# Re-sequencing the opening of a fused retention and GELU-MLP kernel: banks of the state product, weight triggers, who evacuates x

## The chip, the cores and the metric

One core of a Trainium2 chip runs the kernel. The metric is the device time of one execution in microseconds. The records of each execution also give the core's span (first to last instruction, about 1.8 us shorter than the device time here) and the mean clock granted to TensorE, as a share of full speed.

## The reference, cut to what matters

```python
state = gamma * state + k_t v_t^T          # retention, per batch b and head h, 768 steps
y_t   = scale * q_t . state
x = y as (3072 tokens, 512)
h = x @ w_in                               # 512 -> 2048
out = gelu_tanh(h) @ w_out                 # 2048 -> 512
```

Batch 4, 8 heads of 64, 768 positions; fp32 inputs and output.

## The kernel before

The sequence is cut into 6 chunks c of 128 positions. For each chunk and batch b there are pieces of attention, called T, A, Y below, and then the MLP over the four batches together: M1 (`moe1`, 16 column blocks fc, each with a GELU on ScalarE) and M2 (`moe2`).

- T: transposes of scaled q and k on TensorE into a PSUM tile, then a copy to SBUF (`qkT`).
- A: products q k^T, then VectorE multiplies them with the decay mask (`a_sb`).
- Y: the products y = A v (plus q times state for c > 0), and s = k^T v in the same call. y is copied to SBUF as x, s is added to the state `st`, and GpSimd makes the decayed state `stg` for the next chunk.

In the code, `mm_` issues the products of a piece and `ev_` its evacuations from PSUM, `prep1` scales or converts one input, `decay` makes `stg`, and `hold` is a tiny GpSimd copy that waits for a weight and so holds back the loads of chunk 1. In the profiles `h_ps` are the products of M1 and `o_ps` those of M2, "o" and "h" for short.

PSUM is divided into groups of tiles: `att` 3, `o` 2, `h` 3. What the change touches:

```python
    def spin(n):                       # fillers: products of zeros that nobody reads
        ps = psum.tile([128, 512], F32, tag="h", bufs=3, name="spin_ps")
        ...
    def mm_Y(c, b):
        tag, bufs = ("o", 2) if c < 2 else ("att", 3)
        y_ps = psum.tile([128, NHP, 128], F32, tag=tag, bufs=bufs, name="y_ps")
        ...
        if c + 1 < NCk:
            s_ps = psum.tile([128, NHP, 128], F32, tag=tag, bufs=bufs, name="s_ps")
        ...
    # the opening, chunk 0 (cut)
    mm_A(0, 1); ev_A(0, 1); spin(2)
    PO.tensor_copy(out=misc[0:1, 1:2], in_=ld_tile("q", 0, 3)[0:1, 0, 0:1])
    load_w_in(0); load_w_in(1); prep1(PO, "k", 0, 3); load_w_in(2); load_w_in(3)
    mm_T(0, 2); ev_T(0, 2, AC); prep1(AC, "v", 0, 2); prep1(VE, "q", 0, 3)
    mm_Y(0, 1); ev_Y(0, 1, AC); ev_S(0, 0); spin(1)
    mm_A(0, 2); ev_A(0, 2); prep1(AC, "v", 0, 3); spin(3)
    mm_T(0, 3); ev_T(0, 3); mm_Y(0, 2); ev_Y(0, 2, AC)
    mm_A(0, 3); ev_A(0, 3); ev_S(0, 1); spin(1)
    moe1(0, 0, 0, half); moe1(0, 1, 0, half)
    mm_Y(0, 3); ev_Y(0, 3); ev_S(0, 2); ev_S(0, 3)
    for b in range(B): decay(0, b)
    ...
    # chunk 1 (cut)
    run1("T0"); moe1(0, NF - 1); run1("A0"); spin(3); run1("Y0 T1")
    ...
    zip_units(units, pieces(1, "T2 A2 Y2 T3 A3 Y3"))
```

## Time and profile before

| | before |
|---|---|
| median of 3 executions | 231.49 us (231.47 to 232.06) |
| the profiled execution | 233.13 us, span 231.3, clock 0.993 |
| TensorE busy | 219.0 us, 95% |
| slices of the clock row below 0.9 | one, at 11.6 to 17.3 us |

In the page's view of the span in 40 slices, the row for the clock has its only dip in the third slice, in tenths:

```profile
PEclk9979999999999999999999999999999999999999
```

The lines of the chain, the waits and the timelines are shown in the prediction.

### The profile page before, as it was taken

What the parts mean: (1) busy time and instruction counts of PE and PEld (TensorE: products, weight loads), DVE (VectorE), ACT (ScalarE), POOL (GpSimd) and SP (SyncE); (2) the same over time, 40 slices, a digit from 0 to 9 for tenths busy, and PEclk for the clock granted to TensorE, in tenths of its full rate; (3) what the DMA queues carried; (4) which work ended last, traced back from release to release, by engine and by line L of the source; (5) the groups of instructions that cost most, each with busy time, mean ns of one, the idle gap of its engine ahead of it and who ended that gap; (6) DMA issues with size and microseconds to landing.
All of it is one profiled execution on the core that took longest, in us unless ns stands there. A gap on an engine that the chain in (4) does not pass through costs nothing.

```text
span 231.3 us, 4076 instructions
## 1 busy us (share of the span) xinstructions
PE 219.0 (95%) x1669; PEld 119.0 (51%) x1669; DVE 84.1 (36%) x150; ACT 82.6 (36%) x161; POOL 78.7 (34%) x92
## 2 busy tenths in 40 slices
PE   7775999789999999999999999999999999999993
PEld 3434645678744554554544554445544445444453
DVE  3566205773000675645342445342434233200001
ACT  2642664647621111154511154511155412166220
POOL 3582388255940037940666546700000000000000
PEclk9979999999999999999999999999999999999999
DMA  7999799999995782299311199411110011200112
GB/s 178 288 183 206 140 268 254 204 194 235 203 251 163 192 207 89 66 246 204 83 45 48 45 229 253 111 45 48 47 45 3 0 45 50 90 1 0 43 51 91
DMA packets 83011, 29.74 MB, mean 129 GB/s; under 512 B 75568, under 2 KB 80048, under 8 KB 82992
## 3 DMA queue, kind: packets, MB, share of 16 engines
q1 hardware_dynamic: 65776, 17.94, 33.2%
q0 software_dynamic: 4224, 4.19, 11.2%
q10 hardware_dynamic: 12992, 7.34, 10.3%
q8 instruction: 13, 0.21, 0.4%
q14 instruction: 6, 0.05, 0.1%
HBM read 27.37 MB, written 6.29 MB: 146 GB/s over the span
## 4 chain that ended last, share of the span: by engine, by line
PE 86%; DVE 6%; DMA 5%; issue 1%; ACT 0%; SPq 0%; DVEq 0%
PE o_ps L342 36%; PE h_ps L322 35%; PE qkT_ps L175 4%; PE a_ps L193 3%; PE y_ps L228 3%; PE s_ps L240 3%; DMA q<-in_q_dram 2%; DMA k<-in_k_dram 2%; DVE a_sb L206 2%; PE y_ps L218 2%; DVE qkT L169 1%; DVE q L145 1%; PE spin_ps L112 1%; DVE st L259 1%; DVE xT L169 1%
## 5 line engine op out<-in xcount | busy, mean ns | idle before, releaser
L322 PE MATMUL h_ps<-xT,w_in 128*128 128x512 f16 (+2 forms) x504 | 89.7, 328 | 0.5 <-DVE xT L169 0.5
L342 PE MATMUL o_ps<-w_out,g 128*128 128x512 f16 (+1 forms) x400 | 87.8, 371 | 0.0
L331 ACT ACTIVATE g<-h_ps 128x512 f16<-128x512 f32 (+2 forms) x126 | 61.8, 496 | 64.4 <-PE h_ps L322 63.1
L322 PEld LDWEIGHTS <-w_in 128*128 128x128 f16 x504 | 44.7, 98 | 33.4 <-issue 0.6
L342 PEld LDWEIGHTS <-g 128*128 128x128 f16 x400 | 37.6, 98 | 39.0
L206 DVE TENSOR_TENSOR a_sb<-a_ps,mask 128x512 f16<-128x512 f32 x48 | 30.9, 686 | 28.4 <-PE a_ps L193 28.4
L363 ACT COPY o_sb<-o_ps 128x512 f32<-128x512 f32 x18 | 10.6, 586 | 67.2 <-PE o_ps L342 67.2
L268 POOL TENSOR_TENSOR stg<-st,cst 128x512 f32<-128x512 f16 x16 | 16.5, 1040 | 44.8 <-DVE st L259 39.7
L145 POOL TENSOR_TENSOR k<-k,cst 128x512 f16<-128x512 f32 x24 | 25.2, 1049 | 8.6 <-DMA k<-in_k_dram 8.6
L169 DVE CAST xT<-y_ps 128x512 f16<-128x512 f32 x21 | 14.5, 691 | 29.8 <-PE y_ps L228 29.8
L169 DVE COPY qkT<-qkT_ps 128x1024 f16<-128x1024 f16 x21 | 14.5, 692 | 26.4 <-PE qkT_ps L175 26.1
L145 POOL TENSOR_TENSOR q<-q,cst 128x512 f16<-128x512 f32 x20 | 20.9, 1045 | 9.3 <-DMA q<-in_q_dram 9.2
L259 DVE TENSOR_TENSOR st<-s_ps,stg 64x256 f16<-64x256 f32 x32 | 13.4, 418 | 0.5
L360 DVE COPY o_sb<-o_ps 128x512 f32<-128x512 f32 x5 | 3.5, 692 | 26.7 <-PE o_ps L342 26.7
L228 PE MATMUL y_ps<-a_sb,v 128*64 128x128 f16 x192 | 10.8, 225 | 1.9 <-DVE st L257 0.9
L193 PE MATMUL a_ps<-qkT 64*128 64x128 f16 x192 | 9.8, 222 | 2.3 <-DVE qkT L169 1.6
L193 PEld LDWEIGHTS <-qkT 64*128 64x128 f16 x192 | 5.5, 95 | 11.4 <-issue 6.4
L112 PE MATMUL spin_ps<-zero 128*128 128x512 f16 x29 | 10.0, 478 | 1.2 <-DVE zero L104 1.2
L240 PE MATMUL s_ps<-v,k 128*128 128x128 f16 x80 | 8.0, 222 | 2.5 <-DVE st L257 1.0
L175 PEld LDWEIGHTS <-q 128*128 128x128 f16 x96 | 7.3, 100 | 5.8 <-issue 1.0
L142 POOL CAST v<-v 128x512 f16<-128x512 f32 x16 | 9.8, 611 | 0.0
L175 PE MATMUL qkT_ps<-iden,k 128*128 128x128 f16 x96 | 9.5, 223 | 0.2 <-POOL k L145 0.2
(29 smaller groups left out, 73.2 us busy)
## 6 DMA issues: line engine op xcount, KB each, us to landing
k<-in_k_dram SPq DMA_DIRECT2D x22, 256.0 KB, 4.3
q<-in_q_dram SPq DMA_DIRECT2D x22, 256.0 KB, 4.3
v<-in_v_dram SPq DMA_DIRECT2D x18, 256.0 KB, 4.5
out_dram<-o_sb ACTq DMA_DIRECT2D x18, 256.0 KB, 2.0
w_in<-in_moe_w_in_dram POOLq DMA_DIRECT2D x4, 512.0 KB, 8.1
w_out<-in_moe_w_out_dram POOLq DMA_DIRECT2D x4, 512.0 KB, 9.6
v<-in_v_dram ACTq DMA_DIRECT2D x6, 256.0 KB, 4.9
out_dram<-o_sb SPq DMA_DIRECT2D x5, 256.0 KB, 2.1
```

The costliest lines, as they stand in the source:

```text
L145: eng.tensor_tensor(out=t, in0=src, in1=cst[:, col:col + H].unsqueeze(2).broadcast_to([128, H, Dh]), op=ALU.mult,)
L169: eng.tensor_copy(out=out, in_=in_)
L175: nc.tensor.transpose(out=ps[:, i, hp], in_=pair(h16[nm, c, b], hp), identity=iden)
L193: nc.tensor.matmul(out=ps[j][:, hp], lhsT=t[j * 64:(j + 1) * 64, 1, hp], rhs=t[j * 64:(j + 1) * 64, 0, hp], start=True, stop=True,)
L206: nc.vector.tensor_tensor(out=s, in0=ps[j], in1=mask[:, j], op=ALU.mult)
L228: nc.tensor.matmul(out=y_ps[j * 64:(j + 1) * 64, hp], lhsT=vv[:, 2 * hp + j], rhs=a_sb[c, b, j][:, hp], start=(c == 0), stop=True, skip_gr ...
L240: nc.tensor.matmul(out=s_ps[:, hp], lhsT=pair(kk, hp), rhs=pair(vv, hp), start=True, stop=True)
L259: nc.vector.tensor_tensor(out=st[sl, :, b, sl], in0=s_ps[sl, :, sl], in1=stg[sl, :, b, sl], op=ALU.add,)
L268: nc.gpsimd.tensor_tensor(out=stg[:, :, b], in0=st[:, :, b], in1=cst[:, OG:OG + NHP].unsqueeze(2).broadcast_to([128, NHP, 128]), op=ALU.mult,)
L322: nc.tensor.matmul(out=h_ps[:, t0:t1], lhsT=w_in_sb[wi][:, kc, wr * 128:(wr + 1) * 128], rhs=xT[c][:, kc, t0:t1], start=(kc == 0), stop=(k ...
L331: nc.scalar.activation(out=g_sb[c, fc][:, t0:t1], in_=h_ps[:, t0:t1], func=AF.Gelu_apprx_tanh, scale=1.0,)
L342: nc.tensor.matmul(out=ps[:, n0:n1], lhsT=g_sb[c, fc][:, b * C:(b + 1) * C], rhs=w_out_sb[fc // (NF // NO)][:, fc % (NF // NO), n0:n1], st ...
```

## The change

Its intent: TensorE should no longer wait for PSUM banks while it works through chunk 0, the weights should start earlier, and VectorE should be relieved of the x evacuations of chunk 1. The diff, cut:

```diff
-        ps = psum.tile([128, 512], F32, tag="h", bufs=3, name="spin_ps")
+        ps = psum.tile([128, 512], F32, tag="o", bufs=2, name="spin_ps")
...
         if c + 1 < NCk:
+            tag, bufs = (h_b if b < 3 else att_b) if c == 0 else (o_b if c == 1 else att_b)
             s_ps = psum.tile([128, NHP, 128], F32, tag=tag, bufs=bufs, name="s_ps")
...
-    mm_A(0, 1)
-    ev_A(0, 1)
-    spin(2)
-    PO.tensor_copy(out=misc[0:1, 1:2], in_=ld_tile("q", 0, 3)[0:1, 0, 0:1])
     load_w_in(0)
     load_w_in(1)
     prep1(PO, "k", 0, 3)
     load_w_in(2)
     load_w_in(3)
+    mm_A(0, 1)
+    ev_A(0, 1)
+    spin(2)
     mm_T(0, 2)
     ev_T(0, 2, AC)
-    prep1(AC, "v", 0, 2)
+    ev_S(0, 0)
     prep1(VE, "q", 0, 3)
     mm_Y(0, 1)
     ev_Y(0, 1, AC)
-    ev_S(0, 0)
-    spin(1)
+    prep1(AC, "v", 0, 2)
+    prep1(AC, "v", 0, 3)
...                                    # the other spin(1) goes too
-    for b in range(B):
-        decay(0, b)
...
+    decay(0, 0)
+    decay(0, 1)
     hold("q", 1, 0, w_in_sb[2][0:1, 0, 0:1])
+    decay(0, 2)
+    decay(0, 3)
...                                    # y: Y with x on ScalarE; s: state update and decay
-    run1("Y0 T1")
+    run1("y0 T1 s0")
...
-    zip_units(units, pieces(1, "T2 A2 Y2 T3 A3 Y3"))
+    zip_units(units, pieces(1, "T2 s1 A2 y2 T3 s2 A3 y3 s3"))
...
-    zip_units([u for b in range(B) for u in units2(1, b)], std(2))
+    zip_units([u for b in range(B) for u in units2(1, b)], std(2), 15)
```

More of the change, by code (lines that the diff above doesn't have):

```diff
@@ L211, in mm_Y @@
         kk = h16["k", c, b]
-        tag, bufs = ("o", 2) if c < 2 else ("att", 3)
+        att_b, o_b, h_b = ("att", 3), ("o", 2), ("h", 3)
+        tag, bufs = o_b if c < 2 else att_b
         y_ps = psum.tile([128, NHP, 128], F32, tag=tag, bufs=bufs, name="y_ps")
@@ L447 @@
     ev_Y(0, 1, AC)
-    ev_S(0, 0)
-    spin(1)
+    prep1(AC, "v", 0, 2)
+    prep1(AC, "v", 0, 3)
     mm_A(0, 2)
     ev_A(0, 2)
-    prep1(AC, "v", 0, 3)
     spin(3)
@@ L460 @@
     ev_S(0, 1)
-    spin(1)
     moe1(0, 0, 0, half)
@@ L480, with att_y, att_s @@
         load1(SY, "k", 1, b)
+    def att_y(c, b):
+        mm_Y(c, b)
+        ev_Y(c, b, AC)
+    def att_s(c, b):
+        ev_S(c, b)
+        decay(c, b)
+    fn["y"], fn["s"] = att_y, att_s
     def run1(names):
@@ L509 @@
         moe1(1, fc, 0, C)
-    run1("Y1")
+    run1("y1")
     for fc in range(7, 10):
```

## The prediction

> **What bounds the kernel now.** I read the page's busy shares first, then the chain of waits, then who TensorE waited for, then the timelines of TensorE, GpSimd and VectorE in the first 55 us.
>
> ```profile
> span 231.3 us, 4076 instructions
> PE 219.0 (95%) x1669; PEld 119.0 (51%) x1669; DVE 84.1 (36%) x150; ACT 82.6 (36%) x161; POOL 78.7 (34%) x92
> PE 86%; DVE 6%; DMA 5%; issue 1%; ACT 0%; SPq 0%; DVEq 0%
> ```
>
> TensorE is busy 219.0 of 231.3 us and 86% of the chain that ended last is its own. So the change can win only TensorE's idle time, its filler matmuls ("spin", which write nothing that is used) and any time at a slow clock. All three lie early. The waits of TensorE between 11 and 24 us, then its timeline there:
>
> ```profile
> PE s_ps L240 <- DVE st L257: 1.0, 1, 1.0
> PE y_ps L228 <- DVE st L257: 0.9, 1, 0.9
> PE s_ps L240 <- DVE xT L169: 0.8, 1, 0.8
> PE s_ps L240 <- ACT xT L167: 0.7, 1, 0.7
> ```
>
> ```profile
> 12.99 0.38 PE L228 MATMUL y_ps<-a_sb,v 128*64 128x128 f16 x7 [0.29 <-DVE a_sb L206]
> 14.37 0.46 PE L240 MATMUL s_ps<-v,k 128*128 128x128 f16 x4 [0.99 <-DVE st L257]
> ...
> 15.73 1.46 PE L112 MATMUL spin_ps<-zero 128*128 128x512 f16 x3
> ...
> 21.92 0.41 PE L228 MATMUL y_ps<-a_sb,v 128*64 128x128 f16 x8 [0.94 <-DVE st L257]
> 23.11 0.38 PE L240 MATMUL s_ps<-v,k 128*128 128x128 f16 x4 [0.78 <-DVE xT L169]
> ```
>
> The four waits, 3.4 us, are for a bank and not for data: y and s of chunk 0 share two PSUM banks, so each s (or the next y) waits until an earlier one has been evacuated. The clock, by stretch (the column behind the engines' times):
>
> ```profile
> 14.50:18.00 3.50, 3.50 (x26) 1.76 (x25) 1.29 (x2) 0.49 (x1) 3.29 (x4) 0.51 1.10 176
> 11.10:14.50 3.40, 1.99 (x25) 1.06 (x22) 3.19 (x6) 2.40 (x5) 2.22 (x5) 1.00 0.96 209
> 18.00:21.40 3.40, 2.29 (x30) 1.65 (x30) 2.28 (x4) 1.35 (x3) 0.00 (x0) 1.00 1.24 208
> ```
>
> After the stretch with only 1.99 us of matmul TensorE ran at half clock for 3.5 us; after 2.29 us it did not. Then GpSimd, whose order sets when weights start, and two waits further on:
>
> ```profile
> 12.36 0.18 POOL L436 COPY misc<-q 1x1 f32<-1x1 f32 x1 [1.17 <-DMA q<-in_q_dram]
> 12.48 1.69 POOL L302 DMA_DIRECT2D w_in<-in_moe_w_in_dram  x2
> 14.19 1.06 POOL L145 TENSOR_TENSOR k<-k,cst 128x512 f16<-128x512 f32 x1
> ```
>
> ```profile
> 41.36 0.40 PE L193 MATMUL a_ps<-qkT 64*128 64x128 f16 x8 [0.91 <-DVE qkT L169]
> ...
> 96.61 1.02 PE L322 MATMUL h_ps<-xT,w_in 128*128 128x512 f16 x4 [0.48 <-DVE xT L169]
> ```
>
> The weight triggers wait 1.17 us for an input that GpSimd doesn't need. At 41.36 and 96.61 TensorE waits because VectorE evacuated x first.
>
> **What the Trainium skill says.** "TensorE: Matmul & The Clock Gate", section "What's actually happening", gives two clock states, a half-rate one after an idle window of about 3.4 us, and a free-running window. The trace agrees in size: 3.5 us at 0.51, then 1.00. "PSUM — Partial Sum Buffer", "Specifications (TRN2)", gives eight banks of 512 fp32 values per partition, so each s or y tile fills one; the kernel's 3 + 2 + 3 tiles use all eight, so s in the M1 group takes banks that exist. "SBUF — State Buffer", "Terms", says that VectorE and GpSimd share a port pair held by one for a whole instruction. The trace agrees: the q scaling at 10.50 us, beside a k scaling, took 1.24 us on VectorE, against 0.69 alone.
>
> **The change part by part, times on the axis of the old trace.**
>
> (1) s of chunk 0, b = 0 to 2, moves to the h banks (free then), b = 3 to the att banks. Up to y of b = 1 nothing moves: its second half still waits for the mask product that ends at 12.93, and it ends about 13.4. Then s of b = 1 follows at once (0.3) and not at 14.37. The A product of b = 2 can go at 13.65 and not at 15.19, since its transposed copy ended at 13.46.
>
> (2) VectorE now does st of b = 0 (0.85) before q of b = 3 (0.67): 12.93 to 13.78, to 14.43. Then the mask product of b = 2 (1.29): 14.43 to 15.72, where it ended at 17.12. That is 1.4 us earlier.
>
> (3) GpSimd triggers the first two weights at 11.2 (end of the k scaling that began at 10.14) and not at 12.48. The first weights took 5.6 us from issue to landing, so about 16.8. But k of b = 3 was issued at 7.35 and took 6.8, so it lands at 14.15 in either kernel: its scaling stays at 14.2, and may lose 0.2 to q on the shared port, ending at 15.25 to 15.45. So "last k between the triggers" gains nothing by itself; it keeps k from falling behind. The last two weights keep their trigger, but the transfers before them start 1.3 us earlier.
>
> (4) With TensorE denser between 11.1 and 14.5 (s and A move in: about 2.5 us against 1.99, above the 2.29 that kept the clock) I expect no half-clock stretch. The three fillers then take 0.65 us and not 1.46.
>
> (5) The chain from there: k transposes at 15.4 to 15.85; evacuation (0.69) to 16.6; A of b = 3 to 17.0, mask product 17.1 to 18.4. First M1 block (four matmuls of 0.108) at 17.0, if its weights landed. The built program's buffers show that the second and third M1 blocks get the bank of the first again, so each waits for the GELU: 0.43 + 0.2 until it starts + 0.41, about 1.1 us. Second block 18.1, y and s of b = 3 to 19.2, third block 19.2, fourth 19.6 (its bank held s of b = 1, evacuated 18.4 to 19.25), then the second halves 20.3, 20.7, 21.2, 21.6, the full blocks (fc = 4 on) at 22.1. In the old trace the first full block's GELU began at 27.01; less 0.86 of matmul and 0.2 it began at 25.95. Gain 3.85 us. The two single fillers dropped (0.63 and 0.39) are inside this. I take 3.8.
>
> (6) Chunk 1: x evacuations to ScalarE (four of 0.59), s and decay as pieces. VectorE loses 0.69 per b, so A of b = 1 need not wait: copy of T1 at 39.95 to 40.64, A at 40.70 and not 41.36, gain 0.66. But st (0.86) now stands between the transposed copy and the mask product. For b = 2: copy ends 45.62, st 46.48, mask product 47.77, so y's second half at 47.83 against 47.93 of old, after a wait of 1.0. For b = 3: mask product 51.06 to 52.35, y at 52.41; s ends at 53.06 (old 53.5), but three units of 0.43 are left and not two. End 54.35 against 54.38. I take 0.05: the gain is off the path again within the stage.
>
> (7) The end of chunk 2's attention goes one unit (four matmuls, 0.86) earlier, so its last x evacuation (0.69) runs beside that unit: the 0.48 wait goes. I take 0.5.
>
> (8) The decays behind the hold and the earlier weights bring the hold from 25.9 to about 23, and chunk 1's loads and GpSimd scalings about 3 us earlier. TensorE did not wait for those before (k of b = 0 was scaled at 31.2, wanted at 35.23), and with TensorE 3.8 earlier it needs them at 31.4 against 28.2. No gain, no loss.
>
> Sum: 3.8 + 0.05 + 0.5 = 4.35. From 231.49 that gives 227.1 us.
>
> **The rivals.** (a) The M1 start waits for the weights. For it: the DMA engines are full until about 13.5 us, and landings of the later weights took 8.9 to 10.7 us. Against: the first needs about 2.4 us from trigger to its first bytes, so it starts when the inputs end. A landing at 17.8 moves step (5) by 0.8: 227.9. (b) The half-clock stretch comes all the same, or later. For it: the windows are free-running, and step (5) has GELU waits of 0.5. Against: no stretch of 3.4 us there has less than 2.2 us of matmul. It would cost up to half of 3.5, of which I think 0.6 to 1.7 is on the path: 227.7 to 228.8. (c) ScalarE becomes the bound in chunk 1: it was busy 9.5 of 18.1 us, plus 2.4 makes 11.9. Average against it, order for it, as x evacuations queue behind GELUs: 0.3 to 0.6, 227.5. (d) Chunk 1 keeps its 0.66 and more (TensorE reaches the long run of second halves earlier): 226.4.
>
> **Range and chances.** Most errors I can think of (landing, semaphore delays that I left out, ScalarE's order) lengthen; (d) and a faster k landing shorten. Low 225.9, high 228.5. The mark for 2% is 226.9, just under my value: faster 0.40, within 2% 0.59, slower 0.01.
>
> **What would show it.** Step 1: s of b = 1 without its 0.99 wait, no half-clock stretch. Step 3: w_in trigger near 11.2, k of b = 3 still scaled from about 14.2. Step 5: second and third M1 blocks waiting for ScalarE's GELU and not VectorE's st; first full-width GELU near 23.2. Step 6: TensorE waits near 1 us for a_sb in chunk 1 (two of them), and the stage from T0 to the second halves as long as before, 18.1 us. Step 7: no wait at the first h of chunk 2. The prediction is wrong if the M1 blocks wait for w_in, the clock row dips after 18 us, or the gain up to the full blocks is not near 3.8.

## The result

The changed kernel took 228.69 us (median of 4, 228.54 to 229.09) against 231.59 us of the kernel before in the same rounds. The ratio is 0.9874, with a 95% interval of 0.9854 to 0.9893. Ratios here are the mean time of one kernel's fast runs over that of the other's of the same rounds, so not quite the ratio of the medians. So it is 2.9 us faster, under the mark of 2%, where 4.35 us had been forecast, and just outside the range of 225.9 to 228.5.

The traces say something else. The span went from 231.3 to 226.8 us, by 4.5. First the page's lines:

```profile
span 226.8 us, 4071 instructions
PE 218.0 (96%) x1667; PEld 118.3 (52%) x1667; DVE 81.3 (36%) x146; ACT 85.0 (37%) x165; POOL 78.7 (35%) x91
```

TensorE lost 12.3 us of span to other than matmul before (231.3 less 219.0) and loses 8.8 now. TensorE's waits between 11 and 24 us (total, times, longest):

```profile
PE h_ps L324 <- ACT g L333: 0.5, 1, 0.5
PE qkT_ps L175 <- POOL k L145: 0.4, 1, 0.4
PE y_ps L229 <- DVE a_sb L206: 0.3, 1, 0.3
```

The four bank waits of the prediction (3.4 us) are gone. In their place stand 0.4 us for the last k and 0.5 us for the first GELU. The timeline of TensorE at the same places (start, duration, then the instruction and in brackets the idle time before it and what ended it):

```profile
13.18 0.38 PE L229 MATMUL y_ps<-a_sb,v 128*64 128x128 f16 x7 [0.29 <-DVE a_sb L206]
13.50 0.40 PE L242 MATMUL s_ps<-v,k 128*128 128x128 f16 x4
...
14.16 0.82 PE L112 MATMUL spin_ps<-zero 128*128 128x512 f16 x3
...
17.16 0.61 PE L324 MATMUL h_ps<-xT,w_in 128*128 128x256 f16 x4
18.24 0.60 PE L324 MATMUL h_ps<-xT,w_in 128*128 128x256 f16 x4 [0.47 <-ACT g L333]
...
31.66 0.39 PE L175 MATMUL qkT_ps<-iden,q 128*128 128x128 f16 x4
```

s follows y at once, and the three fillers took 0.82 us where they had taken 1.46: they ran at full clock. The last line is T0 of chunk 1; it stood at 35.45 in the profile before. The stretches confirm the clock (busy time of TensorE, weight loads, VectorE, ScalarE, GpSimd, then the clock):

```profile
11.10:14.50 3.40, 3.04 (x41) 1.79 (x41) 3.35 (x6) 2.43 (x5) 1.95 (x4) 1.00 1.26 254
14.50:18.00 3.50, 2.77 (x35) 1.70 (x33) 2.84 (x6) 1.50 (x4) 3.49 (x4) 1.00 1.23 207
```

So the profile shows almost exactly the forecast gain and the timed executions show two thirds of it. The question is where the other 1.5 us are.

### The profile page after: what moved, and what is told of

Same layout as the page of the kernel before. It is cut to its first block, busy times and chain, and to the rows that moved or that the text cites. A ratio compares the mean times of both kernels' runs of the same rounds, so it can differ in the third digit from the quotient of the medians.

```text
span 226.8 us, 4071 instructions
## 1 busy us (share of the span) xinstructions
PE 218.0 (96%) x1667; PEld 118.3 (52%) x1667; DVE 81.3 (36%) x146; ACT 85.0 (37%) x165; POOL 78.7 (35%) x91
## 2 busy tenths in 40 slices
DMA packets 83011, 29.74 MB, mean 131 GB/s; under 512 B 75568, under 2 KB 80048, under 8 KB 82992
## 4 chain that ended last, share of the span: by engine, by line
PE 87%; DMA 3%; DVE 3%; POOL 2%; issue 2%; SPq 1%; ACT 0%; DVEq 0%; POOLq 0%
PE o_ps L344 36%; PE h_ps L324 36%; PE qkT_ps L175 4%; PE y_ps L229 3%; PE a_ps L193 3%; DMA k<-in_k_dram 3%; PE s_ps L242 2%; PE y_ps L219 2%; DVE a_sb L206 1%; SPq L77 1%; DVE qkT L169 1%; POOL k L145 1%; DMA out_dram<-o_sb 1%; POOL w_in L304 1%; DVE st L261 0%
## 5 line engine op out<-in xcount | busy, mean ns | idle before, releaser
L169 DVE CAST xT<-y_ps 128x512 f16<-128x512 f32 x17 | 11.8, 692 | 28.3 <-PE y_ps L229 27.1
L229 PE MATMUL y_ps<-a_sb,v 128*64 128x128 f16 x192 | 11.2, 224 | 1.8 <-DVE a_sb L206 1.7
L112 PE MATMUL spin_ps<-zero 128*128 128x512 f16 x27 | 9.1, 479 | 1.2 <-DVE zero L104 1.2
L229 PEld LDWEIGHTS <-v 128*64 128x64 f16 x192 | 6.7, 108 | 5.5 <-issue 3.2
```

The costliest lines, as they stand in the source:

```text
L169: eng.tensor_copy(out=out, in_=in_)
L229: nc.tensor.matmul(out=y_ps[j * 64:(j + 1) * 64, hp], lhsT=vv[:, 2 * hp + j], rhs=a_sb[c, b, j][:, hp], start=(c == 0), stop=True, skip_gr ...
```

## The experiments

**Theory A.** The half-clock stretch of the kernel before (clock 0.51 from 14.5 to 18.0 us) is in some of its executions only. The profiled one had it, most timed ones do not. The gain from its absence must not be subtracted from the median. **Theory B.** The stretch is in every execution of before, and the 1.64 us come from elsewhere. **Theory C.** The opening gave its 3.8 us everywhere and chunk 1 gave some back. Each kernel was timed in 5 rounds beside the kernel before. "Undisturbed" below means executions with a mean clock above 0.993; I chose this mark after seeing the records of before, which fall into two groups (next paragraph). Five executions in all are labelled slow in the record (over 1.5% above the fastest of their kernel); all five are among the disturbed ones, so no undisturbed figure below holds any of them.

### 1. The kernel before, again

No edit.

> The kernel before, unchanged, timed with clock and span of each execution. Theory A (start of the sum): the profiled execution of before (233.13 us, span 231.3, clock 0.993) was one with a half-clock stretch, and most timed ones have none: most runs here show clock 1.000, spans near 229.7 and 231.5 us; few or none show 0.993 and 233. Theory B: the stretch is in every execution and the 1.64 us between the profiled one and the median come from elsewhere: all runs show a clock near 0.993 whatever their time.

231.65 us median, ratio to before 1.0003. The executions of before that listed clocks, 50 with these six, fall apart: 39 with a clock of 0.997 or more took 231.20 to 232.13 us (median 231.64), 11 with 0.993 or less took 232.99 to 238.66 (median 233.28). Nothing lies between 232.13 and 232.99. The profiled execution of before, 233.13 us at 0.993, is of the second group. The executions ran on four chips, and each has both kinds. The profile of this run is one of the first:

```profile
11.10:14.50 3.40, 1.87 (x23) 1.09 (x21) 3.04 (x6) 2.37 (x5) 2.27 (x4) 1.00 0.98 200
14.50:18.00 3.50, 2.83 (x38) 1.70 (x37) 1.97 (x3) 0.92 (x2) 3.15 (x4) 1.00 1.13 182
```

```profile
12.84 0.38 PE L228 MATMUL y_ps<-a_sb,v 128*64 128x128 f16 x7 [0.29 <-DVE a_sb L206]
14.21 0.40 PE L240 MATMUL s_ps<-v,k 128*128 128x128 f16 x4 [0.99 <-DVE st L257]
...
15.09 0.82 PE L112 MATMUL spin_ps<-zero 128*128 128x512 f16 x3
...
33.97 0.39 PE L175 MATMUL qkT_ps<-iden,q 128*128 128x128 f16 x4
```

Same program, same wait of 0.99 us for a bank, but the clock stays at 1.00 and the fillers take 0.82 us. From y's second half (12.84) to T0 of chunk 1 (33.97) is 21.13 us. In the profiled execution of before it was 35.45 less 12.99, 22.46. So the stretch costs 1.33 us there, and theory B falls.

The single kinds of piece can now be compared with an undisturbed execution, each row as the difference of two starts in the TensorE timelines:

| stage | before, profiled | before, undisturbed | changed |
|---|---|---|---|
| y of b = 1 (second half) to T0 of chunk 1 | 22.46 | 21.13 | 18.48 |
| T0 of chunk 1 to first o | 25.77 | 25.79 | 25.69 |
| first o to first h of chunk 2 | 35.39 | 35.39 | 34.74 |
| sum of gains of the changed kernel | 4.71 | 3.40 | |

Against this stands that y of b = 1 came 0.34 us later in the changed kernel's profile (13.18 against 12.84), while the code before it is the same on TensorE. Less that, the undisturbed sum is 3.06, and the spans give 3.1 (229.9 less 226.8).

The first row must not be read alone, since y of b = 1 starts at a different time in each execution. In the second profile of the changed kernel (experiment 6) it came at 12.57 and T0 at 31.89, so that the row would be 19.32: TensorE was early there and then waited for weights. Counted from the start of the span, T0 of chunk 1 came 2.31 us earlier than in undisturbed before (33.97 less 31.66), and 2.08 us earlier in the second profile.

### 2. Fillers in the bank wait

```diff
         if c + 1 < NCk:
+            if (c, b) == (0, 1):
+                spin(3)
             s_ps = psum.tile(...)
```

> Before plus three fillers (about 0.65 us) in the 0.99 us in which TensorE waits for the s bank of b = 1, so that the stretch from 11.1 to 14.5 us holds 2.6 us of matmul and not 1.99. Theory A: nothing to gain in the median, 231.3 to 231.7 us, and no run with a clock below 0.999. Theory B: the stretch goes in every run, about 1.6 us faster, 229.9.

231.74 us, ratio 0.9988 (0.9962 to 1.0015), and none of six executions at 0.993 or below (three had 0.997, where none below 0.999 was expected). Nothing is gained in the median, as theory A has it. That six of six kept the clock is weak by itself: with 11 in 50, six clean ones in a row come about one time in four or five (0.78 to the sixth power is 0.23).

### 3. Fewer fillers

```diff
-    spin(2)          # ahead of y of b = 0
     mm_Y(0, 0)
...
     ev_A(0, 1)
-    spin(2)          # behind A of b = 1
```

> The kernel before with two pairs of fillers dropped (ahead of y of b = 0 and behind A of b = 1), about 0.9 us of matmul less in the 6 us before the bank wait; no wait depends on them. Theory A (the stretch comes when a window holds too little matmul): most executions have a clock of 0.993 or less, about 233 us. Rival (the stretch strikes at random, whatever the matmul density): as often as in before, 4 of 17, median 231.6.

233.31 us, and all six executions at a clock of 0.984 to 0.993. The profile:

```profile
11.10:14.50 3.40, 1.61 (x23) 1.10 (x21) 2.69 (x5) 2.91 (x6) 2.61 (x4) 0.99 0.90 202
14.50:18.00 3.50, 3.50 (x30) 1.79 (x27) 1.34 (x3) 0.32 (x1) 3.48 (x5) 0.52 0.97 148
```

So the stretch is not blind to the program: it came in 11 of 50 executions of before (3 of 11 in the same rounds) and in 6 of 6 with fewer fillers, by their clocks. What in the program brings it is not separated: besides the fillers that are gone, s of b = 1 waits 1.32 us for a bank here, not 0.99, so a thinner use of TensorE and a longer gap both changed.

### 4. The opening alone, and the rest alone

The opening alone is the change with chunk 1 and chunk 2 as before:

```diff
-    run1("y0 T1 s0")
+    run1("Y0 T1")
...
-    zip_units(units, pieces(1, "T2 s1 A2 y2 T3 s2 A3 y3 s3"))
+    zip_units(units, pieces(1, "T2 A2 Y2 T3 A3 Y3"))
...
-    zip_units([...], std(2), 15)
+    zip_units([...], std(2))
```

> The change's opening alone (banks, order, weight triggers, decays behind the hold), chunk 1 and chunk 2 as before. Theory A: the opening is worth 2.9 less the 0.5 of chunk 2, so about 2.3 against undisturbed runs of before: 229.2 us. Theory C (the opening is worth its 3.8 and chunk 1 gives 0.9 back): 227.8 us.

229.53 us, ratio 0.9907. Five of six executions are undisturbed with the same median, 2.1 us under the 231.64 of undisturbed before. One had 0.993 and took 231.53, so a slow stretch can still come; whether it comes less often, six executions cannot tell.

The rest alone is the converse edit on the kernel before.

> The rest alone: chunk 1 with x on ScalarE and s as pieces of their own, chunk 2 one unit earlier, opening as before. Theory A with the prediction's steps 6 and 7: 0.05 + 0.5 faster, 231.0 us. Theory C: chunk 1 costs about 0.9, so 0.4 slower, 231.9 us. In both the wait of 0.48 at the first h of chunk 2 is gone in the profile.

231.88 us, ratio 0.9969 (0.9922 to 1.0016), inconclusive as it stands: three of the six executions had 0.990 or less, and two of these are labelled slow. The three undisturbed ones have a median of 230.91, 0.7 us under 231.64. That agrees with the table above (0.10 + 0.65) and with the expectation of 231.0. 2.1 and 0.7 make the 2.8 us that the changed kernel gains in undisturbed executions (median of nine 228.82, against 231.64), and theory C falls.

### 5. Banks alone, triggers alone

```diff
-        ps = psum.tile([128, 512], F32, tag="h", bufs=3, name="spin_ps")
+        ps = psum.tile([128, 512], F32, tag="o", bufs=2, name="spin_ps")
...
+            if c == 0:
+                tag, bufs = ("h", 3) if b < 3 else ("att", 3)
             s_ps = psum.tile(...)
```

> The kernel before with the banks alone changed (s of chunk 0 in the h and att groups, fillers in the y group), every order and trigger as before. Theory A with step 3 (the weights are the next bound): the four bank waits of 3.4 us go, a wait for the first w_in of about 1 us comes in their place, 1.5 us faster on undisturbed runs, 230.1 us. Rival (the banks are all of the opening's gain): 229.2 us and no wait for w_in.

230.70 us; the four undisturbed executions have a median of 230.45, 1.2 us under before. TensorE's waits between 11 and 24 us:

```profile
PE h_ps L324 <- DMA w_in<-in_moe_w_in_dram: 0.9, 1, 0.9
PE h_ps L324 <- ACT g L333: 0.5, 1, 0.5
PE y_ps L228 <- DVE a_sb L206: 0.2, 1, 0.2
```

The bank waits are gone, and the first weights have become the wait, as its expectation had it, though for a gain of 1.2 us and not 1.5. Then the GpSimd part alone:

```diff
-    PO.tensor_copy(out=misc[0:1, 1:2], in_=ld_tile("q", 0, 3)[0:1, 0, 0:1])
...
-    for b in range(B):
-        decay(0, b)
...
+    decay(0, 0)
+    decay(0, 1)
     hold("q", 1, 0, w_in_sb[2][0:1, 0, 0:1])
+    decay(0, 2)
+    decay(0, 3)
```

> The kernel before with the GpSimd part alone: weight triggers without the wait for an input, two decays behind the hold. Banks and orders as before. Theory A (the banks bound the opening, the weights were in time): no faster, 231.5 us on undisturbed runs, w_in triggered 1.2 us earlier. Rival (the triggers are worth something by themselves): 230.5.

231.53 us, all six undisturbed, 0.1 us under before and within noise. My "triggered 1.2 us earlier" was off for this execution: its weights were triggered at 12.06, not 11.1, since its k of b = 2 was scaled only from 11.07 (its input came later). So banks alone give 1.2, triggers alone 0.1, and the opening with both and with its new order 2.1: they are worth more together, since the banks turn the weights into the bound. How much of the remaining 0.8 is the triggers and how much VectorE's and ScalarE's new order was not separated.

### 6. The changed kernel again, and three attempts to go further

> The changed kernel unchanged, for its share of half-clock executions and as the measure for the two kernels that follow. Theory A (opening worth 2.65 on undisturbed runs): 228.5 to 228.8 us for runs with clock above 0.996, and of these nearly all. If the stretch is as frequent as in before (4 of 17 executions at 0.993 or less), one or two of six show it, some 1.4 us longer.

228.93 us, ratio 0.9871 (0.9838 to 0.9903). Five executions at 0.998 or more (228.56 to 229.07), one at 0.985 with 232.67. With the first four, 1 of 10 executions is disturbed, against 11 of 50 of before. That the share fell is not shown: at a share of 11 in 50, one or none in ten comes about one time in three. In this profile TensorE waited for the weights as well:

```profile
17.39 0.61 PE L324 MATMUL h_ps<-xT,w_in 128*128 128x256 f16 x4 [0.77 <-DMA w_in<-in_moe_w_in_dram]
...
31.89 0.39 PE L175 MATMUL qkT_ps<-iden,q 128*128 128x128 f16 x4
```

In the first profile M1 began at 17.16 without such a wait, because attention ran 0.6 us later there (y of b = 1 at 13.18, here at 12.57). The two executions end at 226.8 and 227.0. So attention and weights now end within less than a microsecond of each other, and an earlier attention alone gains little. Waiting is the commoner case: of the seven profiles with the changed opening (the two of the changed kernel, the opening alone and the four kernels below), five wait for the first weights, for 0.68 to 1.20 us. From the first M1 block to T0 of chunk 1 it was 14.50 us in both profiles of the changed kernel and in that of the opening alone.

Then the state update behind the mask product in chunk 1:

```diff
-    run1("y0 T1 s0")
+    run1("y0 T1")
...
-    run1("A1")
+    run1("A1 s0")
...
-    zip_units(units, pieces(1, "T2 s1 A2 y2 T3 s2 A3 y3 s3"))
+    zip_units(units, pieces(1, "T2 A2 s1 y2 T3 A3 s2 y3 s3"))
```

> The changed kernel with each chunk-1 state update put behind the mask product instead of in front of it. Theory A (step 6: st of 0.85 in front of the mask product gives the 0.66 back): the waits of y for a_sb in chunk 1 shrink from 1.2 us to about 0.5, 0.5 to 0.7 us faster than the changed kernel: 228.1. Rival (ScalarE's order bounds chunk 1): the same time, 228.7.

229.47 us; five undisturbed with a median of 229.27: not faster, rather 0.4 slower than the changed kernel in the same rounds (the undisturbed executions of the two overlap; in the profiles T0 of chunk 1 to first o takes 26.10 us against 25.69). My expectation was wrong. The waits of TensorE in chunk 1, first of the changed kernel, then of this one:

```profile
PE y_ps L229 <- DVE a_sb L206: 1.2, 4, 0.4
PE a_ps L193 <- DVE qkT L169: 0.4, 1, 0.4
```

```profile
PE a_ps L193 <- DVE qkT L169: 1.5, 3, 0.6
PE s_ps L242 <- DVE st L261: 0.7, 2, 0.4
PE y_ps L229 <- DVE a_sb L206: 0.2, 1, 0.2
```

The wait for the mask product went, but A now waits more for the transposed copy, because less M1 work lies between T and A (one unit of four matmuls where the changed kernel had three; A of b = 2 and of b = 3 wait 0.6 us each, and there none), and s waits for its bank, which the later state update frees later. The sum grew from 1.6 to 2.4 us. The rival I had named, ScalarE, is in none of these lines. This run's profiled execution was also a disturbed one (231.06 us, 0.993), and its stretch lies later, behind a wait of 1.20 us for the weights:

```profile
15.00:18.40 3.40, 2.10 (x29) 1.39 (x29) 2.78 (x6) 0.71 (x2) 2.49 (x3) 1.00 1.24 206
...
19.20:22.60 3.40, 3.40 (x25) 2.32 (x24) 2.29 (x5) 0.87 (x3) 0.64 (x1) 0.51 1.24 205
```

On top of that, the second M1 block got a bank of its own:

```diff
-    moe1(0, 1, 0, half)
+    moe1(0, 1, 0, half, bank=("o", 2))
+    moe1(0, 2, 0, half)
     mm_Y(0, 3)
...                                    # the third block goes from its old place
```

> That, and the second M1 block in the y group's free bank with the third block ahead of y of b = 3, so that TensorE doesn't wait 0.47 us for the first GELU. Theory: 0.3 to 0.45 us faster than the one before, 227.7. Rival (VectorE's mask product and state evacuations bound the opening's end): no faster, 228.1.

229.06 us, undisturbed median the same: 0.2 faster than the last one, less than expected. Its profile has the wait for the first GELU gone and a wait of 0.73 us for the weights in front of M1. The bank itself did what was expected: from the first M1 block to T0 of chunk 1 it is 14.07 us where the changed kernel had 14.50.

```profile
17.66 1.68 PE L324 MATMUL h_ps<-xT,w_in 128*128 128x256 f16 x12 [0.73 <-DMA w_in<-in_moe_w_in_dram]
```

But M1 began at 17.66 here and at 17.39 in the second profile of the changed kernel, so that T0 came only 0.16 us earlier (31.73 against 31.89). Why the medians show no more than 0.2 stays open; the undisturbed executions of the last kernel alone spread from 228.66 to 229.86.

What is left in chunk 1 is that TensorE has too little other work while VectorE goes through copy, state and mask product. So I gave it some: the last three full-width M1 blocks of chunk 0, which in the changed kernel all but one come before chunk 1, and one of them in place of three fillers.

```diff
-    for fc in range(4, NF - 1):
+    for fc in range(4, 13):
...
+    load1(AC, "v", 1, 3)
...
-    moe1(0, NF - 1)
+    moe1(0, 13)
...
-    spin(3)
+    moe1(0, 14)
     run1("y0 T1 s0")
+    moe1(0, 15)
```

> The changed kernel with the last three full-width M1 blocks of chunk 0 moved into chunk 1: one behind T0, one in place of the three fillers, one ahead of A1. Theory: in chunk 1 TensorE waits for VectorE's loop and does 0.65 us of fillers, so real work there is worth 0.65 + 0.35: 1.0 us faster than the changed kernel, 227.8 us on undisturbed runs. Rival (chunk 1's inputs come too late when T0 is 1.7 us earlier): GpSimd's k of b = 0 is scaled at 29.74, wanted at 29.94; TensorE waits for it and nothing is gained, 228.7.

227.94 us, ratio 0.9825 (0.9792 to 0.9858), six of six undisturbed: 0.9 us under the changed kernel's 228.82 of undisturbed executions, about the 1.0 expected, though the two were not run in the same rounds nor on the same chip. It is faster than the kernel before, on which side of the 2% mark is not settled, and against the changed kernel it was not measured side by side: all six executions lie below all nine undisturbed ones of that kernel (228.54 to 229.09), while before has an undisturbed median of 231.51 on the one chip and 231.64 on the other, but the ratios' intervals overlap. Its waits in chunk 1:

```profile
PE y_ps L229 <- DVE a_sb L206: 1.0, 3, 0.4
PE y_ps L229 <- ACT v L140: 0.3, 1, 0.3
PE h_ps L324 <- ACT g L333: 0.2, 1, 0.2
```

A no longer waits for its copy, and 0.65 us of fillers have become work.

```diff
     # the same, with the third block inside the interleaved units instead
+    units.insert(5, lambda: moe1(0, 15))
```

> The same with the third block between A2 and y2, where the changed kernel waits 0.7 us for the mask product: 0.65 + 0.7 faster, 227.4 us. Rival as before, 228.7; or the wait only moves to the next y, 228.0.

227.99 us, ratio 0.9827. Not better than the one before, where 0.4 was expected; its executions spread from 226.87 to 228.89 at clocks of 0.998 and above. Its profile shows that the block did its work in chunk 1: y of b = 2 no longer waits for the mask product (0.71 us in the changed kernel), and T0 to first o takes 25.94 us against 26.19 in the last profile. Then, in M2, comes a wait that no other profile here has:

```profile
66.04 6.20 PE L344 MATMUL o_ps<-w_out,g 128*128 128x512 f16 x28 [1.23 <-ACT o_sb L365]
```

```profile
65.40 0.59 ACT L365 COPY o_sb<-o_ps 128x512 f32<-128x512 f32 x1 [3.43 <-DMA k<-in_k_dram]
```

TensorE waited 1.23 us for ScalarE's evacuation of an M2 result, and ScalarE had stood idle for 3.43 us, by the profile until a transfer of k had landed. Without that wait this execution would have ended about 0.4 us before the last profile (226.9 less 1.23 against 226.1), which is the gain that was expected. It was seen in one execution; that it is also what spreads the six is not shown, nor why ScalarE waited.

All of these kernels gave correct results.

## Why the prediction was wrong, step by step

**The steps of the schedule held.** Step 1: s follows y at once. Step 2: the mask product of b = 2 began at 14.65 (forecast 14.43, with everything from y of b = 1 on 0.2 to 0.3 late). Step 3: the weights were triggered at 11.32 (11.2) and k of b = 3 was scaled from 14.47 (14.2). Step 5: the second M1 block waited for the GELU in the shared bank (0.47 us; the third, forecast to wait as well, did not), the first block began at 17.16 (17.0), and T0 of chunk 1 came at 31.66 us (35.45 less 3.8 is 31.65); the first full-width GELU began at 23.23, forecast 23.2. Step 6: chunk 1 became 0.10 us shorter (forecast 0.05). The waits for the mask product are in the trace, but smaller than the "near 1 us" I named (0.71 in two parts for b = 2, 0.28 for b = 3). Step 7: the wait of 0.48 is gone and the stage 0.65 shorter (0.5). Step 8: the hold went at 24.2, not 23, and k of b = 0 was scaled by 29.74, not 28.2, still in time. The sum of spans, 4.5, met the 4.35.

**The step that failed is the last one: "From 231.49 that gives 227.1 us."** The term that was mis-sized for the median is step 5's 3.8 us, with step 4 in it. Its end was right (T0 of chunk 1 at 31.66), but its start was read off an execution of 233.13 us, where T0 stood at 35.45, and the difference was taken from a median of 231.49. In an undisturbed execution of before T0 stood at 33.97. So the term measured 2.31 us, and 2.08 in the second profile of the changed kernel. The rest, 1.48 us, is what the profiled execution was late: 1.33 from y of b = 1 on, where the two executions have the same waits and one has the half-clock stretch, and 0.15 before. By their clocks 39 of 50 executions of before had no such stretch. The warning stood in the material: a profiled execution 1.64 us over a median whose own spread was 0.6, with a clock of 0.993. The right sum was 2.08 to 2.31, plus 0.10 and 0.65, so 2.8 to 3.1, hence 228.4 to 228.7; 228.69 was measured.

**Step 4's rule was also wrong.** The stretch it makes denser held 3.04 us of matmul, not 2.5, and in the profiled execution no half-clock stretch came. The fillers' "0.65 us and not 1.46" mixes two measures: 0.65 is start to start, where the old trace has 1.25; 1.46 is first start to last end, where the new one has 0.82. For the rule I took 2.29 us of matmul per 3.4 us as enough and 1.99 as too little. Undisturbed executions had 1.87 (run 1) and 2.07 (triggers alone) in the same stretch and kept the clock; with 1.61 in its one profile (fewer fillers) it fell, as in all six executions by their clocks; and in the kernel with s behind A it fell after a stretch of 2.10. So the amount in one fixed stretch does not decide alone. What decides in a single execution, I did not find out; where the stretch lies against the free-running window that the prediction quotes would fit, and no run shows it.

**The rivals.** (a), M1 waiting for the weights, was real: 0.77 us in one of two profiles of the changed kernel, and hidden in the other. It was one of the prediction's own signs of being wrong. (b), a half-clock stretch all the same, occurred by the clock with the opening alone (1 of 6) and with the changed kernel (1 of 10), its place unknown, and, seen in a trace and later, in the kernel with s behind A. (c), ScalarE as the bound of chunk 1, shows in no wait of the changed kernel there. (d) did not come.

## What to carry to other kernels

Before subtracting gains from a time, check that the profiled execution is a typical one: compare its time and its granted clock with the median's, and if they differ, work out the gain against the typical execution. When two waits are removed in one stage, ask which bound stands behind each: here the banks alone gave 1.2 us and the triggers alone 0.1, but together with the new order 2.1. And where TensorE idled here because VectorE's loop was longer, re-ordering that loop moved the wait, while handing TensorE useful work from elsewhere shortened it.

## What the Trainium skill lacked or had wrong

- "TensorE: Matmul & The Clock Gate", sections "What's actually happening" and "HAM oscillation — how this bites in real kernels": they tie the drop to an idle window, or an idle gap, of about 3.4 us. Here the clock fell to about half (0.51 and 0.52) with no idle gap of TensorE over 0.99 us near it (before) or 1.32 us (fewer fillers), after 3.4 us that held 1.99 and 1.61 us of matmul. The page gives no share of activity below which it falls; with 1.87 and 2.07 us it did not fall.
- The same page, section "What's actually happening", says that the number of cold matmuls at the start varies from run to run, that the ramp is under 1% of a typical span, and that one should not fit to a specific count. The size agrees (233.28 against 231.64 us, 0.7%), but the page speaks of the start. Here a half-clock stretch came in the middle of the opening (14.5 to 18.0 us in the traced execution), in 11 of 50 executions of one program by their clocks, and its 1.64 us are over half of the 2.9 us that were to be judged.
- "DMA: Bandwidth & Descriptors", "Specifications", gives about 1 us to the first byte for transfers that GpSimd issues. In the profile before, the trigger of the first weights began at 12.48 us and took 0.95; the DMA rate was 260 GB/s or more until 13.5 us, 29 to 35 from there to 15.0, and then 170. That puts the first bytes about 2.5 us after the trigger's start and 1.6 after its end, an estimate from half-microsecond stretches.
- No page treats the order of a state update against a mask product on VectorE, which mattered in chunk 1 here: with the update in front TensorE waited 1.6 us in the stage, with it behind 2.4.
